# Linear attention and a feed-forward layer on one core: three wider read-backs of the query factors, tile sizes in multiples of 128 bytes, the first denominators apart, and another written order

## The chip, the cores and the metric

One NeuronCore of a Trainium2 chip runs the whole kernel. The metric is device time in microseconds (us), the median of several executions.

## The reference, cut to what matters

For each of 4 batches and 4 heads, 1088 queries and keys of 32 numbers become 64 features each, and the attention is linear in them. The result, 4352 tokens of 128 numbers, goes through a feed-forward layer with 2048 hidden columns. All of it is float32.

```python
def phi(x):
    a = np.einsum('rd,bhsd->bhsr', S1, x)          # 8 numbers
    b = np.einsum('rd,bhsd->bhsr', S2, x)          # 8 numbers
    return np.einsum('bhsi,bhsj->bhsij', a, b)     # 64 features
q_p, k_p = phi(q), phi(k)
kv  = np.einsum('bhsf,bhsd->bhfd', k_p, v)
z   = np.sum(k_p, axis=2)
out = einsum(q_p, kv) / (einsum(q_p, z) + 1e-06)
h = out @ w_in
y = (s * relu(h)**2 + b) @ w_out
```

## The kernel before, in words

The tokens lie along the free axis in nine tiles, one of 256 (tile 0) and eight of 512. A tile t goes through three stages.

**Features, q{t}.** TensorE multiplies the queries by S1 and S2. Tiles 0 and 1 (`direct_features`) do this with the factors already repeated to 64 rows. Tiles 2 to 8 (`stored_features`) compute each factor once (L322, tile `psa`), copy it to SBUF (`abq`, L109), write it to a DRAM tile `qd` (L329) and read it back in four transfers of 64 partitions, each row eight times: two into `pq` (L336), two into `br` (L339). VectorE then multiplies `pq` by `br` (L342).

**Attention, n{t}** (`attend`). 32 small matmuls (L358) put numerators and denominators of the tile's two halves into two PSUM tiles `psa`; VectorE transposes the denominators (L365), adds EPS (L368), takes the reciprocal (L371), transposes back (L375) and multiplies (L381). The result x is split into a rounded part `xh` (L109) and a rest `xl` (L389), both fp32r.

**Feed-forward** (`ffn`), eight pairs of hidden chunks, called {t}{pair}: 6 matmuls of 512 columns into `hp` (L430: wil and wih with xh, wih with xl), relu (L125 on VectorE or L127 on ScalarE), square (L131 or L133), the split into `uh` (L109) and `ul` (L424, always VectorE), and 6 matmuls into `ops` (L430). I call 6 such matmuls a half pair; tiles 1 to 8 have 128 of them, 768 matmuls in all. In the second half pair the last two matmuls take `ul`. Tile 0 runs in plain fp32: 16 matmuls of 256 or 258 columns on each side, each in two passes.

Beside these, k{b} builds the 64x33 matrix of batch b (L244 to L282), w{x} turns one of eight weight pieces from 8-byte into 4-byte floats and splits it, and L... entries issue loads on SyncE (SP). `z` is a matmul on constants into a PSUM tile that nobody reads.

The order is written out by hand: each word of `ORDER` advances one such generator by one step, and every engine, SP's queue too, executes its instructions in the order in which they were issued. `ON_DVE` lists which of the movable elementwise steps (r relu, q square, u rounding, x, w, k, t, a) run on VectorE; the others run on ScalarE. `hp`, `ops`, `psa`, `u`, `pq` and `br` have two buffers each, `uh` and `ul` three.

SBUF tiles are laid one behind the other, each rounded up to 32 bytes. As built, the weights `wih`, `wil`, `woh`, `wol` start 96 bytes past a multiple of 128, `x`, `xh`, `xl`, `u`, `uh`, `ul`, `pq`, `br` and `qt` 64 bytes past one, and the fp32 weights `w24` on one.

Of the kernel before, what the change touches and what calls it, by code (L numbers as in the profile page):

```python
# [9 lines left out]
F32 = mybir.dt.float32  # L10
# [14 lines left out]
NMAX = 512  # L25
# [15 lines left out]
n1 05 n1 k1 n1 w7 07 w7 05 06 n1 05 06 w0 q2 w2 07 w1 06 k1 07 10 k1 q2 w3 q2 w4 07 10 w2 w3 k1 w4 11 Lq3 07
q2 07 k1 q2 10 k1 07 k1 q2 10 q2 11 w5 w5 k1 10 10 11 k1 k1 w6 12 q2 11 w7 11 k1 12 11 k1 w6 12 w7 13 12 14 13
12 12 13 14 13 n2 13 14 13 n2 14 n2 15 n2 n2 14 14 15 n2 n2 n2 15 n2 16 n2 n2 15 17 16 15 15 16 17 20 16 Lq4
16 17 16 20 17 q3 17 Lk2 Lk2 20 17 q3 20 q3 21 17 20 Lv2 Lv2 17 20 21 q3 q3 21 22 q3 q3 21 23 22 21 21 22 23
24 22 q3 23 25 22 23 22 23 24 23 24 25 24 n3 25 26 24 25 24 25 26 26 n3 25 n3 n3 n3 26 n3 27 n3 Lq5 n3 26 26
27 n3 n3 27 k2 n3 q4 k2 30 27 k2 q4 k2 30 q4 31 27 30 k2 27 k2 q4 30 q4 k2 q4 31 30 q4 27 k2 31 27 30 k2 k2 31
31 k2 31 k2 q4 32 33 32 32 34 33 32 n4 33 32 32 33 34 n4 n4 35 33 34 33 n4 n4 n4 Lq6 n4 34 n4 36 n4 35 34 34
n4 Lk3 Lk3 35 36 37 n4 35 36 Lv3 Lv3 41 35 36 37 35 36 36 37 41 q5 37 42 37 q5 41 q5 37 42 41 41 40 42 q5 q5
37 q5 42 43 q5 40 42 37 k3 40 43 44 k3 40 q6 43 q5 45 q6 40 q6 40 44 k3 41 q6 44 q6 43 q6 42 q6 43 Lq7 44 43
45 44 44 45 q6 n5 45 46 45 45 n5 46 n5 n5 n5 46 n5 47 n5 n5 n5 46 k3 n5 q7 n5 47 50 46 47 k3 46 47 50 q7 51 47  # L50
50 q7 k3 50 47 51 q7 50 50 q7 47 q7 51 q7 k3 47 51 k3 51 51 k3 k3 q7 k3 52 k3 Lq8 53 52 52 54 53 52 n6 53 52
52 53 54 n6 n6 55 53 54 53 n6 n6 n6 n6 54 n6 56 55 n6 54 54 n6 55 56 57 n6 55 56 61 55 56 57 55 56 56 57 61 60
57 57 61 57 60 61 62 61 57 60 57 63 62 60 n7 60 62 60 63 62 62 61 63 n7 63 n7 62 n7 n7 63 63 n7 n7 64 n7 n7 n7
65 n7 64 64 66 65 64 q8 65 67 64 65 64 66 q8 q8 65 65 66 67 q8 70 66 q8 q8 66 67 q8 66 70 67 71 67 70 67 70 71
70 70 67 71 67 q8 72 71 73 71 72 72 71 73 72 n8 73 72 72 73 n8 n8 74 73 73 n8 74 n8 n8 n8 n8 74 75 n8 n8 74 76
# [32 lines left out]
def attn_ffn_kernel(ctx: ExitStack, tc: tile.TileContext, qT, kT, vp, s80, cst, w_in, w_out, outT):  # L88
    nc = tc.nc
    PSUM = bass.MemoryType.PSUM  # L90
    const = ctx.enter_context(tc.tile_pool(name="const", bufs=1))
    p1 = ctx.enter_context(tc.tile_pool(name="p1", bufs=1))
    p2 = ctx.enter_context(tc.tile_pool(name="p2", bufs=2))
# [3 lines left out]
    ps_h = ctx.enter_context(tc.tile_pool(name="ps_h", bufs=2, space=PSUM))  # L97
# [463 lines left out]
```

## Time and profile before

| | us |
|---|---|
| median of 3 runs | 277.29 (274.98 to 278.72) |
| the profiled execution | 276.64 |
| its span, first to last instruction | 274.9 |
| TensorE (PE) busy | 246.5 |
| ScalarE (ACT) busy | 197.7 |
| VectorE (DVE) busy | 178.0 |

The profiled execution lies 1.8 us over its span and 0.65 us under the median. Matmuls are pipelined, so a busy TensorE is not TensorE at its peak: how far apart matmuls start tells more. The granted clock, 1.00 or 0.50 in the rows, is TensorE's, of 2.4 GHz.

### The profile page before, as it was taken

To read this page: it belongs to the slowest core of one execution; us is meant where nothing else is said; L and a number is where in the kernel's file an instruction comes from. 1 tells how busy PE (TensorE), PEld (TensorE's weight loads), DVE (VectorE), ACT (ScalarE), POOL (GpSimd) and SP (SyncE) were. 2 spreads that over 40 slices of the span, in tenths; PEclk is the share of its full clock that TensorE was granted. 3 is DMA by queue.
4 is the path that set the end of the run, shared out by engine and by line. 5 is a ranking of instruction groups with operands and counts; after the bars stand their busy time and mean duration, and the time that the engine had idled before them with its cause. 6 is when DMAs were issued, how large, how long until landed. Compare 5 with 4: busy or idle time off the path is not lost.

```text
span 274.9 us, 4313 instructions
## 1 busy us (share of the span) xinstructions
PE 246.5 (90%) x1729; PEld 182.1 (66%) x1729; DVE 178.0 (65%) x246; ACT 197.7 (72%) x232; POOL 3.6 (1%) x15
## 2 busy tenths in 40 slices
PE   7999993599993999969993999989999997999993
PEld 3658772478782667758762857868877775878771
DVE  3899970666625957178563669359786766875661
ACT  2299995079792589459790848669995986789892
POOL 1002100000000000000000000000000000000000
PEclk9999999599997799979999799999999999999999
DMA  6992148100361004940043510620000151000001
GB/s 191 371 403 116 30 116 168 47 0 2 105 189 42 0 2 114 169 142 0 21 117 102 144 42 23 158 70 0 2 38 0 35 139 38 2 0 38 1 0 38
DMA packets 9811, 22.12 MB, mean 80 GB/s; under 512 B 1088, under 2 KB 3520, under 8 KB 9792
## 3 DMA queue, kind: packets, MB, share of 16 engines
q1 hardware_dynamic: 9792, 21.85, 27.6%
q8 instruction: 13, 0.21, 0.4%
q14 instruction: 6, 0.05, 0.1%
HBM read 18.70 MB, written 3.15 MB: 79 GB/s over the span
## 4 chain that ended last, share of the span: by engine, by line
PE 47%; DMA 27%; ACT 10%; SPq 6%; DVE 6%; issue 3%; ACTq 0%; DVEq 0%
PE ops L430 24%; DMA br<-qd 21%; PE hp L430 20%; DVE ul L424 3%; DMA qd<-abq 3%; DMA raw<-w_out 3%; ACT u L133 3%; PE psa L358 3%; ACT u L127 3%; SPq L336 2%; DVE pq L342 1%; ACT w L115 1%; SPq L339 1%; ACT raw L121 1%; ACT uh L109 1%
## 5 line engine op out<-in xcount | busy, mean ns | idle before, releaser
L424 DVE TENSOR_TENSOR ul<-u,uh 128x1024 fp32r<-128x1024 f32 x64 | 78.1, 1222 | 22.1 <-ACT uh L109 19.8
L127 ACT ACTIVATE u<-hp 128x1024 f32<-128x1024 f32 (+1 forms) x62 | 59.8, 964 | 41.4 <-PE hp L430 27.4
L133 ACT ACTIVATE u<-u 128x1024 f32<-128x1024 f32 (+1 forms) x71 | 71.8, 1011 | 9.4 <-DVE u L125 7.6
L430 PE MATMUL ops<-ul,woh 128*128 128x512 f32 x128 | 43.7, 424 | 19.2 <-DVE ul L424 19.0
L430 PE MATMUL ops<-uh,wol 128*128 128x512 f32 x128 | 53.3, 416 | 0.3 <-ACT uh L109 0.3
L430 PE MATMUL hp<-xh,wil 128*128 128x512 f32 x128 | 52.9, 414 | 0.0
L430 PE MATMUL ops<-uh,woh 128*128 128x512 f32 x128 | 52.0, 407 | 0.0
L430 PE MATMUL hp<-xh,wih 128*128 128x512 f32 x128 | 51.3, 400 | 0.0
L430 PE MATMUL hp<-xl,wih 128*128 128x512 f32 x128 | 51.1, 399 | 0.0
L109 ACT CAST uh<-u 128x1024 fp32r<-128x1024 f32 x40 | 42.0, 1049 | 2.7 <-PE ops L430 0.9
L430 PEld LDWEIGHTS ops<-ul,woh 128*128 128x128 f32 x128 | 24.6, 200 | 28.5 <-DVE ul L424 23.4
L342 DVE TENSOR_TENSOR pq<-pq,br 128x1024 f32<-128x1024 f32 x7 | 8.6, 1226 | 38.3 <-DMA br<-qd 31.4
L430 PEld LDWEIGHTS hp<-xh,wil 128*128 128x128 f32 x128 | 24.6, 192 | 9.9 <-issue 1.8
L430 PEld LDWEIGHTS ops<-uh,wol 128*128 128x128 f32 x128 | 24.9, 195 | 8.5 <-issue 1.5
L430 PEld LDWEIGHTS ops<-uh,woh 128*128 128x128 f32 x128 | 24.9, 195 | 5.6
L430 PEld LDWEIGHTS hp<-xl,wih 128*128 128x128 f32 x128 | 24.5, 191 | 6.0
L430 PEld LDWEIGHTS hp<-xh,wih 128*128 128x128 f32 x128 | 24.6, 192 | 5.3
L109 DVE CAST uh<-u 128x1024 fp32r<-128x1024 f32 x24 | 16.6, 692 | 16.1 <-ACT u L133 16.1
L125 DVE TENSOR_SCALAR u<-hp 128x1024 f32<-128x1024 f32 x10 | 12.2, 1223 | 4.5 <-PE hp L430 4.2
L358 PE MATMUL psa<-pq,st 64*32 64x256 f32 (+3 forms) x336 | 11.3, 364 | 2.9 <-DVE pq L342 2.6
L358 PEld LDWEIGHTS psa<-pq,st 64*32 64x32 f32 x336 | 6.0, 110 | 8.1 <-issue 3.8
L251 DVE TENSOR_TENSOR ph<-kab 128x768 f32<-128x768 f32 (+2 forms) x9 | 11.0, 1223 | 0.2
(61 smaller groups left out, 172.3 us busy)
## 6 DMA issues: line engine op xcount, KB each, us to landing
pq<-qd SPq DMA_DIRECT2D x14, 256.0 KB
br<-qd SPq DMA_DIRECT2D x14, 256.0 KB
qt<-qT SPq DMA_DIRECT2D x8, 256.0 KB
raw<-w_in SPq DMA_DIRECT2D x4, 512.0 KB
raw<-w_out SPq DMA_DIRECT2D x4, 512.0 KB
outT<-ot SPq DMA_DIRECT2D x7, 256.0 KB
vt<-vp SPq DMA_DIRECT2D x3, 330.0 KB
kt<-kT SPq DMA_DIRECT2D x3, 320.0 KB
```

The lines of the kernel that those rows point to most:

```text
L109: (nc.vector.tensor_copy if key in ON_DVE else nc.scalar.copy)(out=out, in_=in_)
L115: nc.scalar.activation(out=out, in_=in_, func=AF.Copy, scale=scale)
L121: nc.scalar.activation(out=out, in_=in_, func=AF.Copy, scale=scale, bias=bias)
L125: nc.vector.tensor_scalar(out=out, in0=in_, scalar1=0.0, scalar2=None, op0=ALU.max)
L127: nc.scalar.activation(out=out, in_=in_, func=AF.Relu)
L133: nc.scalar.activation(out=out, in_=in_, func=AF.Square)
L251: nc.vector.tensor_tensor(out=ph[:, c0:c0 + n].rearrange("p c h i x -> p (c h) i x"), in0=a.unsqueeze(3).broadcast_to([P, H * n, R, R]), i ...
L336: nc.sync.dma_start(out=pq[half].rearrange("p h n -> p (h n)"), in_=rows[r, 0].unsqueeze(1).broadcast_to([R, R, H * M]))
L342: nc.vector.tensor_tensor(out=pq, in0=pq, in1=br, op=ALU.mult)
L358: nc.tensor.matmul(nd[r][32 * h:32 * h + 32, y * M + e0:y * M + e1], st_t[b][64 * r:64 * r + 64, h // 2, h % 2, y], pq[64 * r:64 * r + 64, ...
L424: nc.vector.tensor_tensor(out=ul[:, :, :N], in0=u[:, :, :N], in1=f32(uh[:, :, :N]), op=ALU.subtract)
L430: nc.tensor.matmul(out, w, x, start=(first and k == 0), stop=(last and k == len(terms) - 1))
```

## The change

The two factors of tiles 2 to 8 now come from four matmuls of 32 columns, so that `qd` holds all rows of the first factor and then all of the second. The read-back is three transfers: `pq` over 128 partitions, `br` twice over 64. Paddings of `cst_sb`, `vt`, `rc` and `bias` make their sizes multiples of 128 bytes; `sk` keeps its 320 bytes, so that, as built, the tiles from `sq` to `s_bits`, all weights among them, start 64 bytes past a multiple of 128, and `kt`, `pq`, `br`, `x`, `xh`, `xl`, `u`, `uh`, `ul` and `qt` on one. Tile 0's denominators go to an `hp` tile of their own, in a step before the numerators. The reciprocals are transposed back in one instruction in place of two. `ORDER` and `ON_DVE` are new throughout; 16 words of `ORDER` are `z`, where 21 were.

```diff
+DEN_APART = (0,)
 ORDER = """
-Ls Lk0 Lk0 Lq0 s s Lk0 s Lv0 s Lv0 s z z z z z z z z k0 s s Lv0 z q0 k0 Lcst q0 k0 k0 Lq1 q0 Lw0 k0 Lw1 k0 k0
+Ls Lk0 Lk0 Lq0 Lk0 s s Lv0 s s Lv0 s z z z z z z k0 s s Lv0 k0 Lcst k0 z k0 Lq1 q0 q0 Lq2 k0 q0 Lw3 k0 z k0
...
-CS, CB, CT = 0, 1, 2
+CS, CB, CT = 0, 1, 32
...
-        vt = v_in[b] = p2.tile([P, NCH, H, VW], F32, name="vt")
+        vt = p2.tile([P, 1216], F32, name="vt")[:, :NCH * H * VW]
+        vt = v_in[b] = vt.rearrange("p (c h d) -> p c h d", c=NCH, h=H)
...
         for r in range(2):
-            nc.tensor.matmul(ab[64 * r:64 * r + 64, :M], sq, qT_t[t][:, r * M:(r + 1) * M],
-                             start=True, stop=True, skip_group_check=True)
+            for w in range(2):
+                a = 64 * w + 32 * r
+                nc.tensor.matmul(ab[a:a + 32, :M], sq[:, 32 * w:32 * w + 32], qT_t[t][:, r * M:(r + 1) * M],
+                                 start=True, stop=True, skip_group_check=True)
...
-        rows = qd.rearrange("(r w i h) n -> r w i (h n)", r=2, w=2, i=R)
+        rows = qd.rearrange("(w r i h) n -> w (r i) (h n)", w=2, r=2, i=R)
+        nc.sync.dma_start(out=pq.rearrange("p h n -> p (h n)"),
+                          in_=rows[0].unsqueeze(1).broadcast_to([2 * R, R, H * M]))
+        yield
         for r in range(2):
-            half = slice(64 * r, 64 * r + 64)
-            nc.sync.dma_start(out=pq[half].rearrange("p h n -> p (h n)"),
-                              in_=rows[r, 0].unsqueeze(1).broadcast_to([R, R, H * M]))
-            yield
-            nc.sync.dma_start(out=br[half].rearrange("p h n -> p (h n)"),
-                              in_=rows[r, 1].unsqueeze(0).broadcast_to([R, R, H * M]))
+            nc.sync.dma_start(out=br[64 * r:64 * r + 64].rearrange("p h n -> p (h n)"),
+                              in_=rows[1, R * r:R * r + R].unsqueeze(0).broadcast_to([R, R, H * M]))
             yield
...
+        if t in DEN_APART:
+            den_t = ps_h.tile([P, 2, 512], F32, name="hp")
+            den = [den_t[:, r, :M] for r in range(2)]
+        else:
+            den = [num[r][:, M:2 * M] for r in range(2)]
...
+            if y == 0 or t in DEN_APART:
+                yield
...
-        rr = p1.tile([P, 2, NMAX // 2], F32, name="rr")
-        for r in range(2):
-            nc.vector.transpose(out=rr[:, r, :M], in_=rc[:, r, :C].unsqueeze(2).broadcast_to([P, C, 32]))
-            yield
+        rr = p1.tile([P, NMAX], F32, name="rr")
+        nc.vector.transpose(out=rr[:, :N], in_=rc[:, :2 * C].unsqueeze(2).broadcast_to([P, 2 * C, 32]))
+        yield
...
-    bias = const.tile([P, 1], F32, name="bias")
+    bias = const.tile([P, 32], F32, name="bias")[:, 0:1]
```

ScalarE, before, at the end of tile 0: `abq_497` is the copy that starts tile 2's way through DRAM; the `u` around it belong to tile 0's last pairs.

```order
L127 ACTIVATE u_467<-hp_430 128x2x256
L133 ACTIVATE u_467<-u_467 128x2x256
L109 CAST wih_90<-w24_10_97 128x512
L127 ACTIVATE u_480<-hp_462 128x2x256
L133 ACTIVATE u_480<-u_480 128x2x256
L109 COPY abq_497<-psa_476 128x256
L109 CAST woh_92<-w24_11_98 128x512
L109 CAST wih_90<-w24_20_99 128x512
L127 ACTIVATE u_505<-hp_489 128x1024
L477 COPY bias_94<-ops_376 128x1
```

ScalarE now: the same copy is `abq_291`, and `raw`/`w24` are the weight pieces' first conversions.

```order
L111 COPY kvt0_86<-psa_203 33x256 x2
L111 COPY br_252<-hp_253 128x512
L111 COPY st0_284<-psa_275 128x256
L111 COPY br_252<-hp_264 128x512
L111 COPY abq_291<-psa_279 128x256
L123 ACTIVATE raw1_182<-raw1_182 128x512
L117 ACTIVATE w24_00_95<-raw0_195 128x512
L123 ACTIVATE raw0_195<-raw0_195 128x512
L117 ACTIVATE w24_01_96<-raw1_197 128x512
L123 ACTIVATE raw1_197<-raw1_197 128x512
L117 ACTIVATE w24_10_97<-raw0_216 128x512
L123 ACTIVATE raw0_216<-raw0_216 128x512
```

Tile 2's copy stands before all the feed-forward work of tile 0, where it stood behind its last square.

VectorE, before, in tile 2's feed-forward: `pq_1336` is the product of tile 5's two factors, and each `ul` is what the last two matmuls of a pair wait for.

```order
L109 CAST uh_1324<-u_1295 128x1024
L424 TENSOR_TENSOR ul_1326<-u_1295,uh_1324 128x1024
L109 CAST uh_1343<-u_1322 128x1024
L424 TENSOR_TENSOR ul_1355<-u_1322,uh_1343 128x1024
L248 STREAM_TRANSPOSE kab_1378<-psa_1359 128x320
L109 CAST uh_1380<-u_1353 128x1024
L342 TENSOR_TENSOR pq_1336<-pq_1336,br_1337 128x1024
L424 TENSOR_TENSOR ul_1396<-u_1353,uh_1380 128x1024
L251 TENSOR_TENSOR ph_1358<-kab_1378 128x1280
```

VectorE now, the same product, named `pq_1342`:

```order
L440 TENSOR_TENSOR ul_1351<-u_1321,uh_1347 128x1024
L111 CAST uh_1361<-u_1345 128x1024
L440 TENSOR_TENSOR ul_1374<-u_1345,uh_1361 128x1024
L251 STREAM_TRANSPOSE kab_1389<-psa_1365 128x2x128
L111 CAST uh_1393<-u_1363 128x1024
L254 TENSOR_TENSOR ph_1286<-kab_1389 128x1024
L440 TENSOR_TENSOR ul_1411<-u_1363,uh_1393 128x1024
L127 TENSOR_SCALAR u_1424<-hp_1382 128x1024
L346 TENSOR_TENSOR pq_1342<-pq_1342,br_1343 128x1024
L440 TENSOR_TENSOR ul_1449<-u_1391,uh_1436 128x1024
L440 TENSOR_TENSOR ul_1471<-u_1424,uh_1451 128x1024
```

The product moved down behind a kv product (`ph`), a `ul` and a relu that stand ahead of it now. What TensorE has to do meanwhile, counted in `ORDER` from a tile's factor matmuls (first word of q{t}) to the first matmul that stands behind the product (the last two of a second half pair whose `ul` VectorE issues after it, or the tile's own attention):

| tile | 2 | 3 | 4 | 5 | 6 | 7 | 8 |
|---|---|---|---|---|---|---|---|
| half pairs before | 4 | 8 | 8 | 6 | 7 | 9 | 10 |
| half pairs now | 7 | 15 | 14 | 10 | 10 | 17 | 13 |

Tile 2 has, besides, 2 halves of tile 0 before and all 16 now, tile 3 none before and 2 now; the matmuls of k, n and q that stand in these stretches come on top.

## Rows read from the trace of the kernel before

**Rows 1.** The page: span, busy time by engine, and 40 slices

```profile
span 274.9 us, 4313 instructions
...
PE 246.5 (90%) x1729; PEld 182.1 (66%) x1729; DVE 178.0 (65%) x246; ACT 197.7 (72%) x232; POOL 3.6 (1%) x15
...
GB/s 191 371 403 116 30 116 168 47 0 2 105 189 42 0 2 114 169 142 0 21 117 102 144 42 23 158 70 0 2 38 0 35 139 38 2 0 38 1 0 38
```

**Rows 2.** Who waited for whom: us in total, times, longest us

```profile
DVE pq L342 <- DMA br<-qd: 31.4, 6, 7.6
...
PE ops L430 <- DVE ul L424: 19.0, 6, 7.5
...
PE psa L358 <- DVE pq L342: 2.6, 1, 2.6
```

**Rows 3.** The chain that ended last: start us, us, what, at tiles 2 and 5

```profile
38.41 10.09 DMA br<-qd
...
51.03 1.22 PE ops L430 x2
...
134.83 0.61 PE psa L322 x4
...
135.86 1.70 DMA qd<-abq
137.70 0.60 SPq L336
...
139.61 9.07 DMA br<-qd
148.76 1.23 DVE pq L342
```

**Rows 4.** Stretches: us, busy (x) of PE, PEld, DVE, ACT, POOL, PEclk, DMA share, GB/s

```profile
51.00:55.40 4.40, 4.37 (x10) 3.47 (x11) 2.31 (x3) 0.55 (x1) 0.00 (x0) 0.50 0.00 0
87.60:93.00 5.40, 5.36 (x40) 3.15 (x40) 5.20 (x5) 4.17 (x4) 0.00 (x0) 0.50 0.00 0
120.50:123.70 3.20, 3.20 (x11) 2.48 (x9) 2.82 (x5) 3.14 (x4) 0.00 (x0) 0.50 0.05 19
151.20:154.40 3.20, 3.20 (x8) 2.52 (x9) 3.10 (x3) 2.24 (x3) 0.00 (x0) 0.50 0.52 136
35.30:274.90 239.60, 213.41 (x1354) 160.37 (x1350) 149.55 (x188) 172.83 (x185) 0.00 (x0) 0.96 0.23 60
190.00:225.00 35.00, 35.00 (x179) 27.06 (x178) 26.71 (x33) 30.04 (x32) 0.00 (x0) 1.00 0.12 33
```

**Rows 5.** PE in order of time, at half and at full clock: start us, us

```profile
121.56 0.63 PE L430 MATMUL ops<-uh,wol 128*128 128x512 f32 x1
121.99 0.63 PE L430 MATMUL ops<-uh,woh 128*128 128x512 f32 x1
...
206.76 0.40 PE L430 MATMUL ops<-uh,wol 128*128 128x512 f32 x1
...
208.16 0.40 PE L430 MATMUL ops<-uh,wol 128*128 128x512 f32 x1
```

**Rows 6.** Groups by line, shapes apart: busy us, mean ns of one

```profile
L133 ACT ACTIVATE u<-u 128x1024 f32<-128x1024 f32 x63 | 66.7, 1059 | 9.1 <-DVE u L125 7.6
...
L109 DVE CAST uh<-u 128x1024 fp32r<-128x1024 f32 x24 | 16.6, 692 | 16.1 <-ACT u L133 16.1
...
L180 DVE SCALAR_TENSOR_TENSOR w<-raw,w 128x512 int32<-128x512 int32 x8 | 5.5, 692 | 0.3
L389 DVE TENSOR_TENSOR xl<-x,xh 128x512 fp32r<-128x512 f32 x8 | 5.5, 688 | 1.7 <-ACT xh L109 1.7
...
L131 DVE TENSOR_TENSOR u<-u 128x1024 f32<-128x1024 f32 x1 | 1.2, 1224 | 0.0
```

**Rows 7.** In order of time, before tile 0's feed-forward: DVE, ACT, PE

```profile
11.35 0.43 DVE L113 TENSOR_SCALAR w<-raw 128x512 f32<-128x512 f32 x1 [0.94 <-DMA raw<-w_in]
...
16.34 0.92 PE L430 MATMUL hp<-x,w 128*128 128x256 f32 x3 [0.30 <-DVE x L381]
```

More of the change, by code (lines that the diff above doesn't have):

```diff
@@ L34 @@
 DIRECT = (0, 1)
+DEN_APART = (0,)
 FIRST_F32 = (0, 1, 2, 3, 4, 5, 6, 7)
 ORDER = """
-Ls Lk0 Lk0 Lq0 s s Lk0 s Lv0 s Lv0 s z z z z z z z z k0 s s Lv0 z q0 k0 Lcst q0 k0 k0 Lq1 q0 Lw0 k0 Lw1 k0 k0
-Lw2 Lw3 k0 k0 z k0 k0 q0 q0 z k0 q0 Lw4 q1 k0 w0 k0 w0 q1 Lv1 Lv1 w0 Lw5 k0 q1 Lq2 w0 k0 w1 z z n0 q1 q1 w1 w0
-n0 Lw6 n0 w2 Lk1 n0 n0 w2 n0 n0 n0 Lk1 w3 n0 q1 z z z z z z z z 00 w3 w1 01 Lw7 00 w1 n1 00 w2 w4 w2 00 w4 w3
-01 02 w3 01 w4 03 w5 w5 w4 01 02 w5 02 04 w5 w6 02 03 n1 w6 03 w6 05 04 w6 03 04 n1 w1 06 n1 n1 w7 n1 n1 04 w7
@@ L41 @@
[L41 to L55, printed above, removed]
@@ L56 @@
-75 n8 74 75 74 76 75 77 75 76 75 77 76 76 76 77 77 80 77 77 80 80 81 77 80 82 81 77 80 81 80 82 81 84 81 82 81
-84 82 82 82 84 84 83 84 85 83 83 86 85 83 85 87 83 83 85 86 85 84 86 87 85 86 86 86 87 87 87 87 87 87 87 87
+Ls Lk0 Lk0 Lq0 Lk0 s s Lv0 s s Lv0 s z z z z z z k0 s s Lv0 k0 Lcst k0 z k0 Lq1 q0 q0 Lq2 k0 q0 Lw3 k0 z k0
+Lw0 Lw1 k0 k0 z k0 Lw2 k0 q0 q0 Lw4 q0 k0 Lw6 Lw5 q1 k0 k0 q1 Lq4 k0 q1 q2 k0 q1 Lq3 q1 w3 q2 q1 w3 z n0 n0 n0
+q2 w0 n0 n0 w0 n0 n0 n0 Lk1 w1 w0 z z z z z n1 w1 w0 Lw7 w3 w2 z 00 w2 w1 01 00 w1 Lq6 00 w2 01 00 w2 Lv1 01
@@ new lines @@
+w3 02 w4 n1 w4 n1 01 Lv1 02 n1 w4 w6 03 02 w6 w4 02 03 w5 w3 03 04 q2 w5 w6 03 Lk1 w0 04 q2 w6 q2 05 w5 04 w1
+06 w5 05 w0 04 w6 w7 05 n1 07 n1 06 n1 05 06 n1 w3 n1 k1 w1 w7 q3 07 n1 10 07 w7 Lv3 q3 w7 w4 q3 11 k1 w7 w4
+w5 06 w2 w2 07 10 k1 k1 07 07 12 10 k1 07 k1 q3 k1 10 q3 q3 11 Lk2 k1 Lk2 10 10 k1 Lv2 k1 11 Lv2 12 k1 11 14
+k1 11 12 11 12 w5 q2 14 13 12 14 12 14 13 n2 14 13 15 w6 13 n2 n2 16 n2 13 15 15 n2 13 n2 n2 15 n2 17 w7 16 15
+14 n2 16 17 15 n2 16 q3 20 17 16 Lk3 17 16 20 17 21 20 23 20 Lv3 21 17 20 21 23 22 17 Lk3 21 23 20 17 21 23 21
@@ new lines @@
+22 23 24 22 25 22 24 22 24 22 25 24 23 25 24 24 25 n3 25 25 n3 n3 n3 26 n3 n3 n3 27 26 n3 q4 26 n3 k2 n3 q4
+Lq5 30 27 26 Lq7 q4 26 27 26 k2 30 k2 k2 30 31 k2 q4 27 30 q4 32 30 q4 30 k2 27 k2 32 k2 31 32 27 k2 32 k2 34
+31 27 k2 32 27 31 33 k2 31 34 31 33 34 32 34 33 35 34 33 36 33 35 33 35 q4 36 35 34 35 n4 36 35 n4 36 n4 n4 37
+n4 36 36 n4 37 n4 n4 37 q5 n4 k3 n4 37 41 k3 q5 37 q5 37 41 k3 42 37 41 37 40 q5 42 41 q5 q5 41 42 43 42 40 k3
+42 q7 40 45 k3 43 40 q6 k3 43 44 q6 40 q7 q6 40 45 q7 41 q5 45 43 q6 42 q6 q6 43 45 n5 45 44 43 q7 44 n5 q7 n5
@@ new lines @@
+46 q7 n5 n5 44 n5 47 n5 46 n5 44 n5 k3 46 n5 q6 k3 46 47 50 46 k3 47 k3 44 50 45 50 47 46 50 47 47 50 50 q7 47
+47 k3 51 k3 52 51 51 53 52 51 n6 52 51 51 52 53 n6 54 n6 53 n6 n6 52 55 53 54 n6 52 53 54 56 55 n6 55 53 54 54
+54 55 56 57 55 56 n6 55 57 n6 n6 57 56 62 56 56 57 62 57 61 62 60 61 62 61 64 62 n7 61 60 61 57 60 n7 64 60 63
+Lq8 60 57 60 57 64 63 61 n7 63 n7 n7 n7 62 n7 n7 64 n7 65 n7 64 66 63 65 q8 63 63 66 65 64 q8 66 65 q8 67 66
+66 70 65 q8 65 q8 70 67 67 q8 66 67 70 71 67 70 67 70 72 71 67 71 70 72 67 71 73 72 71 72 71 73 q8 75 72 73 n8
@@ L58 @@
+73 72 75 73 75 n8 74 n8 n8 75 n8 n8 73 74 75 76 74 n8 n8 n8 74 77 76 74 74 76 n8 76 81 77 76 75 77 81 82 77 81
+80 77 81 76 81 80 77 80 82 82 80 85 80 77 83 77 82 82 80 83 85 83 81 83 82 85 84 83 85 86 85 84 84 87 86 84 83
+84 84 86 87 85 87 86 86 87 86 87 87 87 87 87 87
 """
 ON_DVE = frozenset("""
-a8 k11 q25 r25 r33 r36 r50 r53 r56 r65 r71 r73 r85 u13 u16 u17 u20 u22 u31 u37 u40 u41 u42 u43 u57 u60 u61 u62
-u66 u67 u74 u75 u76 u80 u81 u82 u86 w0b w0h w0m w5h w6b w6h x2 x5
+a8 k20 k21 k31 q02 q03 q11 q16 q31 q32 q33 q36 q41 q54 q62 q64 q65 q70 q71 q80 q81 q85 q86 r11 r23 r25 r26 r33
@@ L62 @@
+r45 r52 r70 r81 r85 u11 u14 u21 u22 u26 u30 u35 u40 u41 u42 u47 u52 u54 u55 u56 u57 u60 u61 u62 u63 u65 u66
+u71 u74 u80 u82 u83 u84 u86 w2h w3m w5h w5m w7m x3 x4 x6 x7
 """.split())
 NS = 32 * 2 + 2 * R
-CS, CB, CT = 0, 1, 2
+CS, CB, CT = 0, 1, 32
 NCST = CT + P
@@ L350, in attend @@
         pq = qfeat.pop(t)
-        nd = [ps_a.tile([P, 512], F32, name="psa") for r in range(2)]
+        num = [ps_a.tile([P, 512], F32, name="psa") for r in range(2)]
+        if t in DEN_APART:
[3 more added lines that the diff above has]
+            den = [num[r][:, M:2 * M] for r in range(2)]
         for y in (1, 0):
@@ L357, in attend @@
                             b, e0, e1 = halves[r][k]
-                            nc.tensor.matmul(nd[r][32 * h:32 * h + 32, y * M + e0:y * M + e1],
+                            out = (num, den)[y][r]
+                            nc.tensor.matmul(out[32 * h:32 * h + 32, e0:e1],
                                              st_t[b][64 * r:64 * r + 64, h // 2, h % 2, y],
                                              pq[64 * r:64 * r + 64, h, e0:e1],
-                                             start=(y == 1 and k == 0), stop=(y == 0), skip_group_check=True)
-        yield
-        dt = p1.tile([P, 2, NMAX // 2], F32, name="dt")
-        for r in range(2):
-            nc.vector.transpose(out=dt[:, r, :M], in_=nd[r][:, M:2 * M])
-            yield
-        rc = p1.tile([P, 2, NMAX // 64], F32, name="rc")
-        nc.vector.tensor_scalar(out=rc[:, :, :C], in0=dt[:, :, :M].rearrange("p r (c y) -> p r c y", y=32)[:, :, :, 0],
+                                             start=(k == 0 and (y == 1 or t in DEN_APART)), stop=True,
+                                             skip_group_check=True)
+            if y == 0 or t in DEN_APART:
+                yield
+        dt = p1.tile([P, NMAX], F32, name="dt")
+        if t in DEN_APART:
+            nc.vector.transpose(out=dt[:, :N].rearrange("p (r m) -> p r m", r=2), in_=den_t[:, :, :M])
+            yield
+        else:
+            for r in range(2):
+                nc.vector.transpose(out=dt[:, r * M:(r + 1) * M], in_=den[r])
+                yield
+        rc = p1.tile([P, 32], F32, name="rc")
+        nc.vector.tensor_scalar(out=rc[:, :2 * C], in0=dt[:, :N].rearrange("p (c y) -> p c y", y=32)[:, :, 0],
                                 scalar1=EPS, scalar2=None, op0=ALU.add)
         yield
-        nc.vector.reciprocal(out=rc[:, :, :C], in_=rc[:, :, :C])
+        nc.vector.reciprocal(out=rc[:, :2 * C], in_=rc[:, :2 * C])
         yield
-        rr = p1.tile([P, 2, NMAX // 2], F32, name="rr")
-        for r in range(2):
-            nc.vector.transpose(out=rr[:, r, :M], in_=rc[:, r, :C].unsqueeze(2).broadcast_to([P, C, 32]))
-            yield
+        rr = p1.tile([P, NMAX], F32, name="rr")
+        nc.vector.transpose(out=rr[:, :N], in_=rc[:, :2 * C].unsqueeze(2).broadcast_to([P, 2 * C, 32]))
+        yield
         x = p2.tile([P, NMAX], F32, name="x")
@@ L380, in attend @@
         for r in range(2):
-            nc.vector.tensor_tensor(out=x[:, r * M:(r + 1) * M], in0=nd[r][:, :M], in1=rr[:, r, :M], op=ALU.mult)
+            half = slice(r * M, (r + 1) * M)
+            nc.vector.tensor_tensor(out=x[:, half], in0=num[r][:, :M], in1=rr[:, half], op=ALU.mult)
             yield
```

## The prediction

> **What bounds the kernel now.** The page comes first: TensorE is busy for 246.5 of 274.9 us, VectorE for 178.0 and ScalarE for 197.7 [rows 1], so the two elementwise engines have room and TensorE has almost none. But a busy share hides waits and a slow clock, so next I read the list of waits. There TensorE waits for `ul` for 19.0 us and for the feature product for 2.6 us, and VectorE itself waits 31.4 us for the read-back of `br` [rows 2]. The chain joins the two: the transfer for tile 2 ends at about 48.5 us, VectorE multiplies and only then makes the next `ul`, and TensorE, idle for the longest 7.5 us of the list, goes on at 51.03 [rows 2, 3]. So one late transfer stops VectorE's queue, and what stands behind it there stops TensorE. Last come the stretches behind the four longest of these stops: the granted clock is 0.50 there, which is the 1.2 GHz level, while in 190 to 225 us, where TensorE never waits, it is 1.00, 2.4 GHz [rows 4]. At half clock two matmuls start 0.43 us apart, at full clock six take 1.40, 0.2333 each [rows 5].
>
> TensorE therefore bounds the kernel, plus the stops for the read-back, plus what each stop costs afterwards.
>
> **The change, part by part.** I add against the profiled execution, 276.6 us.
>
> *The order around the read-back.* This is the large term. At tile 5 the way from the factor matmuls to the finished product goes 134.83 to 149.99: 15.2 us, or 14.6 after these matmuls end [rows 3]. A `ul` behind it brings TensorE to 15.7. Six half pairs, at 1.40 each 8.4 us, a projection of k3 and four more matmuls (0.9) stood in that time, some 10.6 us in all, hence a stop of about 5. The new order has 10 half pairs there (14.0) and four small items of 0.6 each: 16.4 us, and what comes then is tile 5's own attention, which needs the product alone. One transfer issue less takes 0.60 off the way [rows 3], so the product is ready at 14.0 and 2.4 us are left over. By the same count tile 6 has about 3.0 left over, tile 8 4.2, tile 4 9.4, tile 3 12.7, tile 7 14.8 and tile 2 17. All stops for the read-back go: 19.0 + 2.6 = 21.6 us. What is late next is the ordinary hand-over of `ul`, which in 190 to 225 us cost TensorE nothing [rows 4].
>
> *The clock.* Without stops of 2.6 to 7.5 us the four stretches at 0.50 go too. They last 4.4 + 5.4 + 3.2 + 3.2 = 16.2 us [rows 4], and at full clock the same matmuls would take 0.2333/0.43 = 0.54 of it. Gain 7.4 us.
>
> *Three reads in place of four.* The bytes are the same. Read-backs took 10.1 and 9.1 us from the last issue [rows 3]; the trace has no read with repeated rows over 128 partitions. From below, a reading that scales with the repeated half transfers that remain (two and one wide one for four) gives three quarters of 9.1, 6.8; from above I take twice the longest, 20, as a row that forbids it is missing. I take 9.1, the nearest. Down to 6.8 nothing is gained, since 9.1 is hidden by the half pairs above; each us over 11.5 comes out at tile 5 first.
>
> *Four factor matmuls in place of two.* They write four different groups of 32 columns, and I take them to cost what the two cost, 0.61 us a tile [rows 3]. If they ran one after the other it would be twice, 7 x 0.6 = 4 us more; if all at once, half, 2 us less.
>
> *The alignment.* For VectorE the trace has both kinds: joining the weights, with the output on a multiple of 128, takes 692 ns, the `xl` subtraction, all 64 past one, 688 [rows 6]. I cost it at nothing there and on ScalarE. For the fp32r matmuls all rows are of one kind, so a bound has to do. At half clock a matmul takes 0.43; half of that is 0.215, but at full clock it takes 0.2333 [rows 5]. The 0.018 us that don't shrink with the clock are the most that a better place can give back, 768 x 0.0183 = 14.1 us. Nothing says that they come from the place of the tiles, and the weights stay off a multiple of 128. For a loss the nearest rows are VectorE's two, 4 ns apart in 690, 0.6%, the tile on the multiple being the slower: 0.6% of 768 x 0.2333 is 1.0 us. I take 0, and keep -14.1 and +1.0 as the ends. The Trainium skill, "TensorE: Matmul & The Clock Gate", section "Wait — 56ns, not 53.3ns?", gives 215.7 ns for 512 columns at full clock; the rows here are 17.6 ns over it, so by that page 768 matmuls have 13.5 us to give. Against the place as the cause speaks "SBUF — State Buffer", section "Specifications (TRN2)" of the same skill: lines of 16 bytes, which all tiles start on already; by it the gain is 0. No row here decides between the two.
>
> *The work moved to VectorE.* 17 squares stand there in place of 1, 29 roundings in place of 24, two xh more and two half squares; the transposes in one piece take some back. 16 x 1.224 + 5 x 0.692 + about 1 make 24 us more on VectorE, 202 in all, and ScalarE gets some 24 less, 16 x 1.059 and the roundings [rows 6]. ScalarE's 0.86 share in 190 to 225 us, with TensorE at work throughout, shows that such a load can be hidden [rows 4]; without that cover it is the third rival below. I take 1.0 us for new short waits, from 0 to that rival's price.
>
> *The beginning.* `w24` piece 0 is now loaded behind tile 2's queries and piece 3, 0.79 MB more. It came at 11.35 us; at the 371 GB/s of that slice [rows 1] it comes 2.1 us later, at 13.5. Two conversions on ScalarE and two joins on VectorE, some 2.6 us, end at 16.1, and TensorE began tile 0 at 16.34, when x was ready [rows 7]. x itself comes a little sooner through the denominators' own tile (one transpose for two, about 0.2). The two meet at the same time; I take +0.3, from -0.6 to +2.1 (the whole delay of the load). Five words `z` less stand where TensorE had nothing else to do: 0.
>
> **Sum.** 276.6 - 21.6 - 7.4 + 0 + 0 + 1.0 + 0.3 = 248.9. The profiled execution lies 0.65 below the median; I leave that out, as it is within the spread of the runs, and say 248.5.
>
> **The rivals.**
>
> *The matmuls get faster too.* If the 0.018 us go with the new places, TensorE's work shrinks by up to 14.1 us. VectorE's 202 us then stand beside some 234, so I count on four fifths: 248.5 - 11 = 237.5. For it: the excess is the same in every fp32r matmul of the trace. Against it: nothing else in the rows depends on the place.
>
> *VectorE becomes the bound.* In the densest long stretch without a wait of TensorE it was busy for 26.71 of 35.0 us, 0.763 [rows 4]. If it can't be driven higher, its 149.6 us after 35.3 and the 24 new ones take 173.6/0.763 = 227 us: 35.3 + 227 + 1.8 = 264. Against it: on average a half pair's elementwise work now has more matmuls ahead of it than before, 8.6 us to 6.6 by the same count.
>
> *The read-back gets much longer, and the kernel slower.* Place: the product on VectorE in tiles 5, 6, 8, 4. Price: what the read takes over 9.1 us, less the 2.4, 3.0, 4.2 and 9.4 us left over there. With 12 us more, 21 in all, the stops add up to 9.6 + 9.0 + 7.8 + 2.6 = 29, as much as is saved; beyond that it is slower, say 285 at 14 more. Against it: the longer of the two reads shown took 10.1 [rows 3].
>
> *The change doesn't do what it says.* If another load on SP's queue, in order, keeps the reads late, the stops stay: 272 to 280. Against it: SP issues two tiles' reads back to back only for tiles 6 and 7, and tile 7's product is needed 17 half pairs on.
>
> **How the numbers follow.** Forecast 0.67, own range 244 to 255 (below: factor matmuls 2 less, the beginning 0.9 less, no new waits; above: factor matmuls 4 more and the beginning 1.8). Faster matmuls 0.23, at 234 to 244. VectorE the bound 0.06. Stops stay 0.02, longer read-back 0.02. From 234 to 257 I leave out 0.1 to 0.2. A measurement of this kernel tells about 2% from no change, that is 271.7 to 282.8: faster 0.96 (the first three), within 0.02, slower 0.02.
>
> **What would show it.** Right: TensorE's wait for `ul` under 4 us in all; VectorE's wait for `br` close to 0; the clock at 1.00 from tile 1 on; VectorE busy for about 202 us, ScalarE 173; tile 0 begun between 15.7 and 18.4 us; six matmuls in 1.40 us. Wrong: six matmuls in 1.30 or less (second case), or waits of TensorE for `ul` spread over many pairs with VectorE busy in all of them (third), or a chain that still runs through `br`.

## The result, and the profile after

The changed kernel takes 241.0 us (median of 4 runs, 240.11 to 241.27), the kernel before on the same chip 278.0 (274.98 to 278.94). The ratio is 0.868, 95% interval 0.861 to 0.875. The forecast was 248.5, the range 234 to 257. Faster was right, the size was 7.5 us short: 241.0 lies outside the forecast's own range of 244 to 255, in the range given to the first rival, faster matmuls (234 to 244).

The page of the kernel after: span, busy time, slices of the granted clock, and the chain that ended last.

```profile
span 239.5 us, 4351 instructions
...
PE 233.2 (97%) x1752; PEld 178.7 (75%) x1752; DVE 201.2 (84%) x262; ACT 174.5 (73%) x206; POOL 3.9 (2%) x15
...
PEclk9999999999999999999999999999999999999998
...
PE 95%; DVE 2%; DMA 1%; ACT 1%; issue 0%; ACTq 0%; DVEq 0%
```

Against [rows 1] VectorE gained 23 us of work and ScalarE lost 23, as counted; TensorE's busy time fell by 13 us on nearly the same matmuls. The chain, which went through transfers and VectorE at tiles 2 and 5 [rows 3], is now TensorE's for 95% of the span.

The first line is from the waits of the kernel before, the others from those of the kernel after: us in total, times, longest us.

```profile
DVE ul L424 <- ACT uh L109: 19.8, 19, 3.7
```

```profile
ACT u L129 <- DVE ul L440: 14.6, 15, 3.2
...
DVE ul L440 <- ACT uh L111: 10.2, 12, 1.9
...
DVE pq L346 <- DMA br<-qd: 1.9, 1, 1.9
```

VectorE's wait for the read-back fell from 31.4 us in six waits to 1.9 in one [rows 2]. (A seventh wait of before, 6.9 us at tile 4's product, the profile puts to a `vt` load, but the last part of `br` landed at 117.81 and the product started at 117.93.) TensorE's waits for `ul` (19.0) and for the product (2.6) are gone; the longest that its matmuls have left is 0.8 us. What waits now is ScalarE for `ul`, at most 3.2 us at a time, and VectorE for ScalarE's roundings, 10.2 us in all where it was 19.8.

Stretches of the kernel after, columns as in [rows 4].

```profile
20.00:40.00 20.00, 19.46 (x133) 15.13 (x134) 19.64 (x36) 18.13 (x32) 2.47 (x6) 1.00 0.60 181
40.00:60.00 20.00, 20.00 (x185) 16.29 (x181) 19.36 (x25) 17.24 (x21) 0.00 (x0) 1.00 0.61 157
60.00:235.00 175.00, 175.00 (x1159) 137.03 (x1158) 150.10 (x178) 128.62 (x134) 0.00 (x0) 1.00 0.18 50
190.00:225.00 35.00, 35.00 (x180) 27.92 (x179) 29.76 (x34) 29.07 (x30) 0.00 (x0) 1.00 0.08 26
```

From 40 to 235 us TensorE is never without work and its granted clock is 1.00, the 2.4 GHz level; the four stretches at 0.50 of [rows 4] have no successor there. VectorE is at work for 19.64 and 19.36 of 20 us in the first two stretches, and TensorE is idle for 0.54 us in them.

Tile 5, where the margin was counted as the smallest. VectorE, in order of time:

```profile
123.54 1.22 DVE L440 TENSOR_TENSOR ul<-u,uh 128x1024 fp32r<-128x1024 f32 x1
124.86 1.23 DVE L127 TENSOR_SCALAR u<-hp 128x1024 f32<-128x1024 f32 x1
126.16 1.22 DVE L346 TENSOR_TENSOR pq<-pq,br 128x1024 f32<-128x1024 f32 x1
128.15 2.36 DVE L440 TENSOR_TENSOR ul<-u,uh 128x1024 fp32r<-128x1024 f32 x2 [0.77 <-ACT uh L111]
```

And TensorE: tile 5's four factor matmuls (x8, each in two passes), its attention, and nine matmuls at full clock further on.

```profile
111.78 0.64 PE L327 MATMUL psa<-qt,sq 128*32 128x256 f32 x8
...
128.32 0.63 PE L446 MATMUL ops<-ul,woh 128*128 128x512 f32 x2
128.88 1.09 PE L368 MATMUL psa<-pq,st 64*32 64x256 f32 x32
...
205.77 0.39 PE L446 MATMUL hp<-xh,wil 128*128 128x512 f32 x1
...
207.83 0.39 PE L446 MATMUL ops<-uh,wol 128*128 128x512 f32 x1
```

The product is ready at 127.38 and its attention starts at 128.88 without idle time: 1.5 us are left over. The four factor matmuls take 0.64 us, where two took 0.61 [rows 3]. The last two rows stand nine matmuls apart, 2.06 us or 0.2289 each, where [rows 5] had 0.2333.

ScalarE's copy of tile 5's factors and SP's queue, with the write (L334), an output (L502) and the three reads:

```profile
113.67 0.36 ACT L111 COPY abq<-psa 128x256 f32<-128x256 f32 x1
```

```profile
114.06 0.33 SPq L334 DMA_DIRECT2D qd<-abq  x1
116.78 0.34 SPq L502 DMA_DIRECT2D outT<-ot  x1
117.22 0.55 SPq L339 DMA_DIRECT2D pq<-qd  x1
117.83 1.23 SPq L343 DMA_DIRECT2D br<-qd  x2
```

The last lands at 126.03, 8.8 us after the first issue; tiles 4 and 8 take 8.5. Before it was 11.0 at tile 5 (137.70 to 148.7 [rows 3]). Tile 6, beside whose reads those of tile 7 are issued, still takes 10.6, and there VectorE has its one wait of 1.9 us.

### The profile page after: what moved, and what is told of

Same layout as the page of the kernel before. It is cut to its first block, busy times and chain, and to the rows that moved or that the text cites. A ratio compares the mean times of both kernels' runs of the same rounds, so it can differ in the third digit from the quotient of the medians.

```text
span 239.5 us, 4351 instructions
## 1 busy us (share of the span) xinstructions
PE 233.2 (97%) x1752; PEld 178.7 (75%) x1752; DVE 201.2 (84%) x262; ACT 174.5 (73%) x206; POOL 3.9 (2%) x15
## 4 chain that ended last, share of the span: by engine, by line
PE 95%; DVE 2%; DMA 1%; ACT 1%; issue 0%; ACTq 0%; DVEq 0%
PE ops L446 41%; PE hp L446 40%; PE psa L368 4%; PE psa L268 4%; PE psa L247 2%; PE psa L327 2%; PE hp L307 1%; PE psa L283 1%; PE ops L512 1%; DMA s_raw<-s 1%; DVE w L187 0%; ACT u L129 0%; DVE pq L316 0%; ACT ot L500 0%; DVE rr L390 0%
## 5 line engine op out<-in xcount | busy, mean ns | idle before, releaser
L440 DVE TENSOR_TENSOR ul<-u,uh 128x1024 fp32r<-128x1024 f32 x64 | 77.9, 1221 | 12.7 <-ACT uh L111 10.2
L129 ACT ACTIVATE u<-hp 128x1024 f32<-128x1024 f32 (+1 forms) x62 | 60.0, 968 | 30.4 <-DVE ul L440 14.6
L135 ACT ACTIVATE u<-u 128x1024 f32<-128x1024 f32 (+1 forms) x53 | 53.6, 1012 | 8.7 <-DVE u L127 7.3
L446 PE MATMUL hp<-xh,wil 128*128 128x512 f32 x128 | 51.5, 402 | 0.0
L446 PE MATMUL ops<-uh,wol 128*128 128x512 f32 x128 | 51.1, 400 | 0.0
L446 PE MATMUL ops<-uh,woh 128*128 128x512 f32 x128 | 50.2, 392 | 0.0
L446 PE MATMUL hp<-xh,wih 128*128 128x512 f32 x128 | 50.1, 392 | 0.0
L111 ACT CAST uh<-u 128x1024 fp32r<-128x1024 f32 x35 | 36.5, 1048 | 6.5 <-DVE u L133 3.3
L446 PE MATMUL ops<-ul,woh 128*128 128x512 f32 x128 | 39.9, 393 | 0.0
L111 DVE CAST uh<-u 128x1024 fp32r<-128x1024 f32 x29 | 20.0, 691 | 4.0 <-ACT u L135 3.1
L133 DVE TENSOR_TENSOR u<-u 128x1024 f32<-128x1024 f32 (+1 forms) x19 | 22.1, 1164 | 0.2
L254 DVE TENSOR_TENSOR ph<-kab 128x768 f32<-128x768 f32 (+2 forms) x9 | 11.0, 1221 | 0.2
L368 PE MATMUL psa<-pq,st 64*32 64x256 f32 (+3 forms) x320 | 10.2, 345 | 0.5 <-DVE x L397 0.5
```

Source lines behind the costliest of these rows:

```text
L111: (nc.vector.tensor_copy if key in ON_DVE else nc.scalar.copy)(out=out, in_=in_)
L129: nc.scalar.activation(out=out, in_=in_, func=AF.Relu)
L133: nc.vector.tensor_tensor(out=out, in0=in_, in1=in_, op=ALU.mult)
L135: nc.scalar.activation(out=out, in_=in_, func=AF.Square)
L254: nc.vector.tensor_tensor(out=ph[:, c0:c0 + n].rearrange("p c h i x -> p (c h) i x"), in0=a.unsqueeze(3).broadcast_to([P, H * n, R, R]), i ...
L368: nc.tensor.matmul(out[32 * h:32 * h + 32, e0:e1], st_t[b][64 * r:64 * r + 64, h // 2, h % 2, y], pq[64 * r:64 * r + 64, h, e0:e1], start= ...
```

## The experiments

### The tiles' places

`e1_no_padding` takes all paddings back and keeps the rest. `e2` to `e4` and `e12`, `e13` shift the tiles by wider constants:

```diff
# e1
-CS, CB, CT = 0, 1, 32
+CS, CB, CT = 0, 1, 2
# ... and vt, rc, bias in the sizes of before
# e2 (sk 96, s_bits 96), e3 (sk 88, s_bits 104), e4 (s_bits 96), e12 (sk 96, s_bits 192), e13 (s_bits 112)
-    sk = const.tile([P, NS], F32, name="sk")
+    sk = const.tile([P, 96], F32, name="sk")[:, :NS]
```

> The changed kernel with the four paddings taken back: weights 96 bytes past a multiple of 128 and activations 64 past, as in the kernel before; order, reads and all work as in the changed kernel (241.0 us, six fp32r matmuls in 1.375 us, 229 ns each). If the place of the tiles is what took 4 ns off each matmul (weights or moving operand), matmuls are 233 ns apart again and the time is 244, 768 x 0.004 = 3.1 us more. If the 4 ns came from something else (fewer waits, less traffic beside the matmuls), 229 ns and 241.

> The changed kernel with sk and s_bits padded to 384 bytes, so that the weights too lie on a multiple of 128 (64 past it in the changed kernel). If the weights' place costs matmul time, the spacing falls below 229 ns, by up to the 13 ns that are left over 215.7, 10 us in all, so 231 to 240 us. If only the moving operand's place counts, or no place, 229 ns and 241.

> Weights 96 past a multiple of 128, as before the change, and activations on one, as after it. If the weights' place made the difference, 233 ns and 244 us; if the moving operand's, 229 ns and 241.

> Weights 64 past a multiple of 128, as after the change, and activations 64 past too, as before it. If the moving operand's place made the difference, 233 ns and 244 us; if the weights', 229 ns and 241.

> The changed kernel with the weight tiles on multiples of 512 bytes and the tiles that the matmuls read as moving operand on multiples of 512 too. So far: 229 ns a matmul only where the weights stood at 64 above a multiple of 128 and the moving tiles on a multiple of 512; 232.5 with the pairs (multiple of 512, 128 above one) and (64 above a multiple of 128, 64 above a multiple of 512); 233 to 234 with weights at 96 above a multiple of 128. If the moving tile's own place decides (a multiple of 512): 229 ns or less, 240.5 to 241.5 us. If the distance between the two places decides (64 modulo 128): 232.5 ns, 243.5 us. If both tiles read from one place modulo 512 meet in a bank: more than 234 ns.

> The changed kernel with the weight tiles where they are and the moving tiles 128 bytes further, on a multiple of 128 but not of 256. If the moving tile's place decides: 232.5 ns a matmul, 243.5 us. If the distance to the weights' place, 64 modulo 128, decides: 229 ns, 241 us.

The table has the bytes past a multiple of 512 at which the weights and the moving tiles (`xh`, `xl`, `uh`, `ul`) start as built, and the mean distance between starts of 512-column matmuls, over all of a profile (some 670 to 720) that start less than 0.26 us apart.

| kernel | weights | moving | ns | median us | ratio, 95% interval |
|---|---|---|---|---|---|
| before | 352 | 64 | 233.3 | | 1 |
| e1 | 352 | 64 | 233.2 | 244.19 | 0.888, 0.884 to 0.891 |
| e3 | 480 | 128 | 234.2 | 244.72 | 0.890, 0.886 to 0.894 |
| e2 | 0 | 128 | 232.7 | 243.58 | 0.886, 0.882 to 0.890 |
| e4 | 448 | 64 | 232.5 | 243.53 | 0.885, 0.881 to 0.889 |
| e13 | 448 | 128 | 233.3 | 243.43 | 0.882, 0.877 to 0.887 |
| after, once more (e11) | 448 | 0 | 229.3 | 241.15 | 0.870, 0.867 to 0.874 |
| e12 | 0 | 0 | 227.9 | 240.40 | 0.871, 0.866 to 0.876 |

> The changed kernel itself once more, on the chip of the next three runs. Its six-matmul groups were spaced 229 ns a matmul where the kernel before had 233, and the four variants with other places of the tiles, on one other chip, all had 232.5 to 234. If the places of the changed kernel make its matmuls quicker: 229 ns again, about 240.5 to 241.5 us. If 229 belonged to that one chip or execution: 232 to 234 ns, 243 to 245 us.

TensorE at full clock in e13, seven matmuls apart, then in e12, nine apart:

```profile
206.55 0.39 PE L446 MATMUL hp<-xh,wil 128*128 128x512 f32 x1
...
208.18 0.40 PE L446 MATMUL hp<-xh,wih 128*128 128x512 f32 x1
```

```profile
205.72 0.39 PE L446 MATMUL hp<-xh,wih 128*128 128x512 f32 x1
...
207.76 0.62 PE L446 MATMUL ops<-ul,woh 128*128 128x512 f32 x2
```

1.63/7 is 0.233, 2.04/9 is 0.227. After e1 to e4, run beside each other, had all shown 232.5 or more, the quick matmuls could have been one execution's; e11, run beside other kernels, says they are the changed kernel's; e6, e8, e9 and e10, which keep its places, have 229.3 to 229.7 too, and e5, with the places of before, 233.2. e13 moves the moving tiles by 128 bytes and leaves the weights, and loses all 4 ns; e12 changes the distance between weights and moving tiles and keeps them quick. So the moving tiles' own place decides and not its distance to the weights', and what acted was that the paddings happened to put it on a multiple of 512. Every tile laid behind `s_bits` moves with them in these runs; that it is the moving tiles, and not another of these, is argued from their being what the matmuls read, and no run moves them alone. A multiple of 128, which the sizes aim at, gives nothing (e2, e13). Multiples of 256 were not tried. The weights' place seems to matter for about 1.4 ns (229.3 to 227.9, one profile of e12). e12 against e13, on one chip, is the places of both alone: 3.0 us, intervals apart. e12 may be the better kernel by about 1 us (768 times 1.4 ns is 1.1); the runs can't tell it from the changed one.

### The order and the reads, each alone

`e5_old_order_new_reads` is the kernel before with the three reads and four factor matmuls of the diff alone; `e6_new_order_old_reads` is the changed kernel with the four reads and two matmuls that the diff removes.

> The kernel before with its own order and division between engines, with the three wider reads and the four factor matmuls alone. If the stops went because of the new order: the read that ends last ends some 2.6 us earlier (8.5 against 11.1 us) while the stops of tiles 2 to 8 were 2 to 5 us each, so they become shorter and do not go: 8 stops times up to 2.6 us, with the half clock behind some of them gone, 262 to 268 us. If the wider reads alone carry the change: 241 to 245. If they do nothing: 275.

> The changed kernel with the reads of before (four reads of 64 partitions, two factor matmuls of 64 columns), in the new order. If the order alone hides the read-back: the same time as the changed kernel on this chip, within 0.7 us, with VectorE's wait for the factors read last under 3 us in all. If the margin that the order leaves (2.4 us at tile 5, 3.0 at tile 6, by count) is used up by the 2.6 us that the reads are longer: stops at tiles 5 and 6 of under 1 us each and +1 to +3 us.

e5: 262.53 us (260.19 to 262.78), ratio 0.945 (0.939 to 0.950), inside what was expected. Its waits:

```profile
DVE pq L344 <- DMA br<-qd: 24.3, 7, 6.0
...
PE ops L432 <- DVE ul L426: 10.2, 3, 5.9
```

e6: 242.42 us (241.41 to 243.21), ratio 0.875 (0.872 to 0.878), 1.3 us over the changed kernel on the same chip. Tile 5's product in e6, and TensorE behind tile 6's:

```profile
127.31 1.22 DVE L346 TENSOR_TENSOR pq<-pq,br 128x1024 f32<-128x1024 f32 x1 [2.06 <-DMA br<-qd]
```

```profile
141.43 0.62 PE L446 MATMUL ops<-ul,woh 128*128 128x512 f32 x2
142.09 0.50 PE L446 MATMUL ops<-uh,wol 128*128 128x512 f32 x1
...
142.90 0.40 PE L446 MATMUL ops<-uh,woh 128*128 128x512 f32 x1
143.42 0.73 PE L446 MATMUL ops<-ul,woh 128*128 128x512 f32 x2
```

The product starts 1.15 us later than in the changed kernel, while TensorE is 0.5 ahead there (it could start the attention at 128.36, in the changed kernel at 128.88); it goes on 0.3 late. That is the margin of 1.5 used up. From 141 to 146 us TensorE starts some matmuls 0.43 and 0.52 apart, 1.3 us in all: there the product of tile 6, which ends at 139.72 in place of 138.40, delays the `ul` behind it. So the reads are worth 14.6 us in the old order and about 1.3 in the new one; everything else (order, division and places, of which the places 3) is worth 34.7 with the old reads. The two remove the same stops; their gains do not add.

### A longer read-back

```diff
+        spare = p1.tile([P, 2, 1024], F32, name="spare")
+        for k in range(2):
+            for r in range(2):
+                nc.sync.dma_start(out=spare[64 * r:64 * r + 64, k],
+                                  in_=rows[1, R * r:R * r + R].unsqueeze(0).broadcast_to([R, R, H * M]))
```

> The changed kernel with four more reads of half a factor into a spare tile that nothing uses, queued ahead of the real ones, so that the read-back lasts some 7.6 us longer (about 16 us from its first issue against 8.5). If the order leaves only the margins counted from the kernel before (2.4 us at tile 5, 3.0 at tile 6, 4.2 at tile 8, more elsewhere), stops of 2 to 4 us come back at tiles 5, 6 and 8 and half clock behind them: 248 to 252 us. If the margins of the changed kernel are larger than 7.6 us: the time stays within 1 us of the changed kernel's. With the two wider and earlier reads of 2.6 us undone the time rose by 1.3 us, which speaks for the first.

The shortest of six runs took 262.28 us, the median 268.99 (up to 271.23), against 276.69 for the kernel before on that chip; even the shortest is more than either theory said. The profile, and all that follows, is of it. Its slices of the clock, and TensorE's waits:

```profile
PEclk9999999999999999999995999999999997799999
```

```profile
PE psa L373 <- DVE pq L351: 12.0, 2, 6.9
PEld psa L373 <- issue: 9.5, 9, 7.4
...
DVE pq L351 <- DMA br<-qd: 24.8, 5, 8.6
```

And the chain at tiles 5 and 8:

```profile
122.92 13.42 DMA br<-qd
137.79 1.96 PE psa L373 x32
...
202.59 14.23 DMA br<-qd
218.23 1.96 PE psa L373 x32
```

The four extra issues cost SP 2.6 us before the real reads start, so that the factors landed 8.4 (tile 5) and 9.5 us (tile 8) later against TensorE's progress, not 7.6. TensorE stopped for 6.9 and 5.1 us there: the margins are 8.4 - 6.9 = 1.5 at tile 5, which the changed kernel shows directly, and 9.5 - 5.1 = 4.4 at tile 8. At tile 4 TensorE did not stop, and at tile 6, behind tile 5's stop, it had short waits only. The attention after a stop takes 1.96 us in place of 1.09: half clock again (0.52 from 137.8 to 142.6). The first theory holds, above its price. Of the 21 us between this profile and the changed kernel's some 13 are stops (these two and one of 1.1 at tile 3), about 5 half clock, the rest short waits. The other five runs took 268.11 to 271.23, at a mean granted clock of 0.955 to 0.968 against 0.974; what sets them apart is not shown.

### The division between VectorE and ScalarE

`e10_old_division` replaces `ON_DVE` of the changed kernel by that of before, and nothing else.

> The changed kernel's order, reads and places, with the kernel before's table of which operations VectorE takes: some 24 us of work go back from VectorE to ScalarE. If the order alone does it and neither engine is near its limit: within 1 us of the changed kernel. If the division is part of it: ScalarE with 198 us of work in 241 comes late with the activations at single places, TensorE stops of 1 to 3 us each at some tiles, 244 to 252 us.

257.04 us (256.37 to 258.42), ratio 0.931 (0.926 to 0.936), 16 us over the changed kernel. Page and waits:

```profile
PE 240.6 (94%) x1752; PEld 175.1 (69%) x1752; DVE 176.7 (69%) x236; ACT 196.2 (77%) x232; POOL 3.2 (1%) x15
```

```profile
DVE ul L439 <- ACT uh L110: 39.5, 20, 5.7
...
PEld ops L445 <- DVE ul L439: 11.2, 22, 1.2
```

No stop of TensorE lasts longer than 1.2 us. It is many short ones: VectorE waits 39.5 us for ScalarE's roundings, where the changed kernel has 10.2, and `ul` is late in 22 pairs. The read-back has little part: VectorE waits 2.5 us for it. So the new order removes the long stops with the old division too. The second theory's mechanism is right (ScalarE late at single places), but its stops are smaller and far more, and the price lies above its range. This order was made together with the new division; what an order made for the old one would give was not tried.

### The beginning

```diff
-Ls Lk0 Lk0 Lq0 Lk0 s s Lv0 s s Lv0 s z z z z z z k0
+Ls Lk0 Lk0 Lq0 Lk0 s s Lv0 s s Lv0 s z z z z z z z z k0
```

> The changed kernel with the eight opening matmuls on zeros of before in place of six. In the changed kernel the granted clock rose at 9.4 us, in the kernel before at 4.2. If the two matmuls made the difference: the clock rises at 4 to 5 us, the first projection's and factors' matmuls take half the time, and the end comes up to 2 us earlier, 239 to 240.5 on a chip where the changed kernel takes 241. If the beginning is set by the loads and by VectorE and ScalarE: no difference, within 0.5 us.

240.98 us (239.93 to 242.32) against 241.15: no difference. The granted clock of the stretches can't tell when it rose here: it reads 1.00 from 0.7 to 3.7 us in both profiles, where `z` start 0.42 us apart, and later `z` start 0.22 apart. The second 16 matmuls of the key projection tell more, in the changed kernel, in e9 and in e6:

```profile
5.42 0.87 PE L247 MATMUL psa<-kt,sk 128*32 128x96 f32 x16
```

```profile
5.25 0.54 PE L247 MATMUL psa<-kt,sk 128*32 128x96 f32 x16
```

```profile
4.87 0.54 PE L247 MATMUL psa<-kt,sk 128*32 128x96 f32 x16
```

They were slow in the changed kernel's profile and quick in e9's, as the expectation had it. But e6 has them quick with six opening `z`, and so have e4, e10 and e13, so the two `z` are not shown to be the cause. Nor does it matter at the end: TensorE starts tile 0 at 18.20 in the changed kernel, at 17.81 in its second profile (e11) and at 18.04 in e9, in each when VectorE has joined a weight piece:

```profile
18.20 1.59 PEld L446 LDWEIGHTS hp<-x,w 128*128 128x128 f32 x8 [0.32 <-DVE w L183]
```

So it is the weight pieces and VectorE that set it, as the second theory said.

The denominators' own tile was not tried alone.

## Why the prediction was right, and short

The mechanism of the large terms was right: the stops and the half clock behind them went, for the reason given. The time lies within the stated range only because that range took in the first rival's; the forecast's own range missed it by 3 us, for two small terms of the sum were wrong at once, the short waits and the alignment.

Worked out from the starts of all 768 matmuls of 512 columns in the two profiled executions (276.64 and 241.27, so 35.4 us), each distance less the full-clock distance of its own kernel:

| term | forecast | measured |
|---|---|---|
| stops behind the read-back (six of over 1 us) | -21.6 | -22.2 |
| half clock behind them (32 matmuls, one attention) | -7.4 | -7.8 |
| short waits of TensorE | +1.0 | -2.6 |
| distance of matmuls at full clock | 0 | -2.9 |
| start of tile 1's feed-forward | +0.3 | +0.4 |
| not placed | | -0.3 |
| sum | -27.7 | -35.4 |

**Order and stops: right.** Six stops before, none after, and the cause is the order (e6 with the old reads, e10 with the old division: no stop over 1.2 us). The margin by count was 2.4, 9.4 and 4.2 us at tiles 5, 4 and 8; measured it is 1.5 (profile), 10.0 (product possible at 96.2, attention at 106.21) and 4.4 (e8). The count was good to a us, at tile 5 partly by luck. TensorE's side came out: 16.46 us from the end of the factor matmuls to the attention (112.42 to 128.88) for 16.4. But the product is ready after 15.0 in place of 14.0, and that is the sum of two errors: the read takes 7.6 us from its last issue and not 9.1, and the way to that issue takes 2.5 more, as the copy stands behind a rounding on ScalarE and the reads behind an output in SP's queue (116.78). The fourth rival's mechanism was there, too small to matter. With the reads of before the margin at tile 5 is nothing (e6). Tile 6's 3.0 was not measured.

**Clock: right.** 7.8 for 7.4, and e8 brings the half clock back together with the stops.

**Three reads at nothing: nearly.** They end some 2.5 us sooner, 7.2 to 7.6 from the last issue at tiles 4, 5 and 8, which is nearer to the lower bound of 6.8 than to 9.1. e6 prices them at 1.3 us, not 0: "Down to 6.8 nothing is gained" does not hold, above all for the `ul` behind tile 6's product. **Four factor matmuls at nothing: right**, 0.64 us for a tile where L322's two took 0.61 [rows 3].

**New short waits, +1.0: wrong in sign, 3.6 us.** The step took the 24 us moved to VectorE as a load to be hidden and looked at the busy shares. But `ul` of the kernel before was often late because of ScalarE: VectorE waited 19.8 us for its roundings, now 10.2. e10 shows what hangs on the division: under the new order the old one takes 16 us more, nearly all in short waits. How much of the 2.6 us gained against the kernel before is the division's and how much the order's is not shown. The third rival (VectorE the bound, 264) is refuted: VectorE was busy for 19.64 of 20 us with TensorE idle for 0.54.

**The alignment at 0: wrong, 2.9 us.** Its bounds, -14.1 to +1.0, held it. "Nothing says that they come from the place of the tiles" was the choice between two ends that were far apart; e12 and e13 show that the place of the moving tiles is worth 4 to 5 ns of a matmul. The Trainium skill, "SBUF — State Buffer", section "Specifications (TRN2)", would have made it 0, since all tiles start on its lines of 16 bytes; the measurement differs and decides. The 215.7 ns that the Trainium skill gives in "TensorE: Matmul & The Clock Gate", section "Wait — 56ns, not 53.3ns?", were not reached by any place tried; 227.9 is the lowest. The first rival, 237.5 at 1.30 or less for six, was that mechanism at the full price: six took 1.38, between its sign and the forecast's 1.40. Of its 11 us it had 3.

**The beginning: right in size, by another way.** Tile 0's feed-forward starts at 18.20 in place of 16.34 [rows 7], 1.9 us later and not 0.3. It waits for the join of a weight piece, which stands behind tile 0's x on VectorE, where it waited for x before. But tile 1's attention, 1.29 us, now stands ahead of it, and by 32 us all but 0.4 is made up.

## What to carry to other kernels

Count for each transfer what the bound engine still has to do between its start and its first user, and put more work there before making the transfer shorter: here the order, with its division, was worth some 32 us with the old reads, the shorter reads alone 14.6, and on top of the order 1.3. When elementwise work is moved, ask who waits for each of the two engines at single places; busy shares of 65 and 72% said nothing of the 16 us that hang on the division (e10). And look at where the moving operands of matmuls start: 64 bytes of padding ahead of them were worth 1% here (e4 against the changed kernel).

## What was not expected of the hardware

At full clock a 512-column fp32r matmul starts 227.9 to 229.3 ns after the one before when its moving tile is on a multiple of 512 bytes in SBUF, and 232.5 to 234.2 at 64 or 128 bytes past one. At half clock the place makes no difference: 426.7 ns before (moving tiles 64 past) and 426.7 in e8 (on a multiple), the mean of 26 and 13 distances. VectorE shows nothing of the kind: the `ul` subtraction took 1222 ns before and 1221 after. Of the 0.018 us that the prediction found not to shrink with the clock, the best place gives back 0.0054, some 30%; what the rest is stays open. The `z`, bf16 matmuls of 512 columns on one constant tile, start 217 to 220 ns apart at full clock in every profile (226 or 227 from the first to the second of a row). Here are five of them in the changed kernel:

```profile
14.83 1.26 PE L512 MATMUL ops<-const-bfloat16-1.0 128*128 128x512 bf16 x5
```

So some 8 ns more than the `z` stay with the fp32r matmuls at their best place; whether that is the type, the changing weights or the operands is not shown.
